# Attention with a gated mixer: the output projection of a head group moved into the next group, partial products added up in SBUF

## The chip, the core and the metric

One core of a Trainium2 chip. The metric is device time in microseconds (us); the kernel before takes 1070.64 us, the median of three runs (1069.9 to 1074.41). Engines: TensorE (PE in the profile, its weight loads PEld), VectorE (DVE), ScalarE (ACT), GpSimd (POOL), and SyncE (SP), which issues most DMAs.

## What is computed

The input x has 2048 tokens of 448 features. Two branches are mixed by a gate per token:

```python
g = sigmoid((x * gate_w).sum(-1))
q = (x @ wq) as 16 heads of 28;  k = x @ wk;  v = x @ wv      # one k and v for all heads
a = concat_heads(softmax(q k^T / sqrt(28)) v) @ wo
h = gelu(layernorm(x) @ w1), its four quarters shifted by +1, -1, +2, -2 tokens
x1 = x + h_shifted @ w2
b = x1 + gelu(layernorm(x1) @ w3) @ w4
out = g * a + (1 - g) * b
```

## The kernel before

All arithmetic is kept near fp32 by splitting operands into a high and a low part (names ending in h and l): a product then takes three matmuls, high x high, high x low and low x high.

The work comes in stages. First k, v, the first two q and the mixer (to line 391), then the MLP (lines 393 to 450), then attention (from line 454), where this change lies. At the start of that last stage `gg` holds the gate g, and `x1` is scaled in place to (1 - g) * b (line 596).

**Units.** Attention runs over 16 groups `u` (NU = NB * NG): 4 blocks `b` of 512 query tokens, and in each 4 groups `g` of 4 heads. A group takes 16 key tiles `kt` of 128 keys; `k = u * 16 + kt` counts all of them. For each k the loop at line 646 issues four score matmuls ("s", line 663), one per head, each followed by ScalarE's exponential into SBUF ("p", line 665). After each odd k two tiles' worth of p, from two and three steps earlier, go through the "pv" matmuls (line 625), four heads side by side in one PSUM bank. The softmax sums come out of the same matmuls, from a column of ones beside v. So the loop repeats in pairs of key tiles: eight s, then a block of eight pv (sixteen in the trace, which records each twice).

**The order on TensorE** is written out by hand (`manual_schedule` for PE, line 59); the other engines' order is left to the scheduler. Side work is put between the score matmuls as *jobs*: generators in a list, of which `pump()` (line 601) advances the current one by one step, mostly one matmul, after every second score matmul (four times a pair), or after every one in the last group.

- `q_job(u + 2)` (line 493): eleven matmuls for the queries two groups ahead, put at the head of the list at kt = 2 (kt = 7 in group 0).
- `max_part`, `max_end`, `max_rows` for group u + 1 (called directly at kt 6 to 11): "m", four small matmuls that estimate each row's maximum, reduced by the DVE (line 167), and the small "mt" (line 193).
- When a group's pv is done (at kt = 1 of the next), `recip_begin` copies it to SBUF (o), fetches its sums through a DMA (rt), takes the reciprocal on the DVE and sends it to `rb` by two DMAs. `norm_job` (line 541) is queued for k + 6, counted from the group's last kt: a matmul "rbc" (line 543) spreads the reciprocals over the partitions, the DVE multiplies (line 545), and POOL splits the result into onh and onl (lines 548 and 549; five buffers each, "onh" and "onl").
- After the last group of a block, four `wo_job`s (line 567), one for each 128 tokens, are queued for k + 8. Each adds up the block's output projection in **one PSUM tile** over all four groups, 4 x 3 matmuls ("wo", `wo_group`, lines 556, 558, 560); then `gate_out` (line 562) does out = psum * g + x1 on the DVE (line 564) and stores it.
- The last block is different. Its groups 0 and 1 are queued at the start of the last group (line 650) and its group 2 at its middle (line 632), into four PSUM tiles `wo_last` that stay open to the end; two of them take banks of the score tiles, so that in the last group `s_tile(n, True)` goes round three banks and not five (line 478). Its group 3 is done in the tail (`tail_c`, line 708).

**PSUM banks.** Eight: two "mm", two "s" and one "misc" hold score tiles; one "mx" holds pv; two "m" (`misc_tile` = `m_tile`, line 466) are shared by m, mt, q, rbc and wo. A tile waits until the reader of the bank's earlier tile is done.

The branch at line 734 recomputes everything if a softmax sum came out too large; it isn't entered here.

Of the kernel before, what the change touches and what calls it, by code (L numbers as in the profile page):

```python
# [8 lines left out]
F32 = mybir.dt.float32  # L9
F32R = mybir.dt.float32r  # L10
AF = mybir.ActivationFunctionType
ALU = mybir.AluOpType
# [3 lines left out]
P = 128  # L16
S = 2048
D = 448
# [4 lines left out]
NB = S // 512  # L23
NT = S // P
NF = F // P
NG = H // 4
# [9 lines left out]
def f32(ap):  # L36
    return ap.bitcast(F32)
# [3 lines left out]
def gated_mix_kernel(  # L41
# [13 lines left out]
    nc = tc.nc  # L55
# [11 lines left out]
    x1 = keep.tile([P, NT, D], F32, name="x1")  # L67
# [3 lines left out]
    gg = keep.tile([P, NT], F32, name="gg")  # L71
# [20 lines left out]
    def misc_tile(name):  # L92
        return psA.tile([P, 512], F32, tag="misc", bufs=1, name=name)
# [59 lines left out]
    NU = NB * NG  # L153
# [4 lines left out]
    def max_tile(name):  # L158
        return psA.tile([P, 512], F32, tag="mx", bufs=1, name=name)
# [294 lines left out]
    with tc.tile_pool(name="s3", bufs=1, reuse_waits="tile") as s3, \  # L454
# [8 lines left out]
        woh = s3.tile([P, 4, D], F32R, name="woh")  # L463
# [11 lines left out]
        def s_spare(name):  # L475
            return psA.tile([P, 512], F32, tag="misc", bufs=1, name=name)

        def s_tile(n, last=False):
            return (mm_tile, mm_tile, s_spare, s_more, s_more)[n % (3 if last else 5)](f"s_{n}")

        xact = {}

# [31 lines left out]
        on_of = {}  # L514
# [24 lines left out]
            return o, rb  # L539

        def norm_job(u, o, rb):
            ps = (mm_tile if u == NU - 2 else misc_tile)(f"rbc_{u}")
            nc.tensor.matmul(ps, sel8, rb, start=True, stop=True)
            on = s3.tile([P, 512], F32, tag="onf", bufs=2, name=f"on_{u}")
            nc.vector.tensor_mul(on, o, ps)  # L545
            onh = s3.tile([P, 512], F32R, tag="onh", bufs=5, name=f"onh_{u}")
            onl = s3.tile([P, 512], F32R, tag="onl", bufs=5, name=f"onl_{u}")
            nc.gpsimd.tensor_copy(onh, on)  # L548
            nc.gpsimd.tensor_tensor(onl, on, f32(onh), ALU.subtract)
            on_of[u] = (onh, onl)  # L550
            yield

        def wo_group(ps, b, t, g, first, last):
            tok = slice(t * P, (t + 1) * P)
            onh, onl = on_of[b * NG + g]
            nc.tensor.matmul(ps, onh[:, tok], woh[:, g, :], start=first, stop=False)  # L556
            yield
            nc.tensor.matmul(ps, onh[:, tok], wol[:, g, :], start=False, stop=False)  # L558
            yield
            nc.tensor.matmul(ps, onl[:, tok], woh[:, g, :], start=False, stop=last)  # L560

        def gate_out(n, ps):
            ot = s3.tile([P, D], F32, tag="ot", bufs=3, name=f"ot_{n}")
            nc.vector.scalar_tensor_tensor(ot, ps, gg[:, n:n + 1], x1[:, n, :], op0=ALU.mult, op1=ALU.add)  # L564
            nc.sync.dma_start(out[0, n * P:(n + 1) * P, :], ot)

        def wo_job(b, t):
            ps = misc_tile(f"wo_{b}_{t}")[:, 0:D]
            for g in range(NG):
                yield from wo_group(ps, b, t, g, g == 0, g == NG - 1)  # L570
                if g < NG - 1:
                    yield
            gate_out(4 * b + t, ps)
            yield

        wqraw = s3.tile([P, 4, 512], F32, tag="raw", bufs=2, name="wqraw")
        nc.sync.dma_start(wqraw, wq)
# [20 lines left out]
        jobs = []  # L598
# [13 lines left out]
        def drain():  # L612
            while current[0] is not None or jobs:
                pump()
# [3 lines left out]
        def pv_group(k):  # L618
            u, kt = divmod(k, NT)
            if kt == 0:  # L620
                pv_of[u] = max_tile(f"pv_{u}")
            pv = pv_of[u]
            ps = p_of.pop(k)
            for j in range(4):
                nc.tensor.matmul(pv[32 * j:32 * j + 32, :], vext[:, kt, :], ps[j],  # L625
                                 start=(kt == 0), stop=(kt == NT - 1), tile_position=(0, 32 * j))
            if kt == NT - 1 and u < NU - 1:
                o, rb = recip_begin(u, pv_of.pop(u))
                delayed.append((k + 6, lambda: norm_job(u, o, rb)))
                if u == NU - 2:  # L630
                    for t in range(4):
                        delayed.append((k + 10, lambda t=t: wo_last_job(t, NG - 2)))
                elif u % NG == NG - 1:
                    for t in range(4):
                        delayed.append((k + 8, lambda t=t: wo_job(u // NG, t)))

        wo_last = []

        def wo_last_job(t, g):
            if g == 0:  # L640
                wo_last.append((m_tile if t < 2 else s_more)(f"wo_{NB - 1}_{t}")[:, 0:D])
            yield from wo_group(wo_last[t], NB - 1, t, g, g == 0, False)
            yield

        delayed = []
        for k in range(NU * NT + LAG):
            u, kt = divmod(k, NT)
            while delayed and delayed[0][0] <= k:
                jobs.append(delayed.pop(0)[1])
            if k == (NU - 1) * NT:  # L650
                for g in range(NG - 2):
                    for t in range(4):
                        jobs.append(lambda t=t, g=g: wo_last_job(t, g))
            if k < NU * NT:
                if kt == (7 if u == 0 else 2) and u + 2 < NU:
                    jobs.insert(0, lambda u=u: q_job(u + 2))
                if kt == 8 and (u + 3) % NG == 0 and u + 3 < NU:
                    load_x((u + 3) // NG)
                p_of[k] = []
                for j in range(4):  # L660
                    n = 4 * k + j
                    ps = s_tile(n, u == NU - 1)
                    nc.tensor.matmul(ps, kS[0:98, kt * P:(kt + 1) * P], q_of[u][0:98, j, :], start=True, stop=True)  # L663
                    p = s3.tile([P, 512], F32, tag="p", bufs=4 * (LAG + PVB) + 2, name=f"p_{n}")
                    nc.scalar.activation(p, ps, AF.Exp, scale=SCALE)  # L665
                    p_of[k].append(p)
                    if j % 2 == 1 or u == NU - 1:
                        pump()
                if u + 1 < NU:
                    if 6 <= kt < 10:  # L670
                        max_part(u + 1, kt - 6, m_tile)
                    elif kt == 10:
                        max_end(u + 1)
                    elif kt == 11:
                        max_rows(u + 1, m_tile)
            if k >= LAG and k % PVB == PVB - 1:
                for kk in range(k - LAG - PVB + 1, k - LAG + 1):
                    if kk >= 0:
                        pv_group(kk)
        assert not delayed  # L680
        drain()

        u = NU - 1
        pv = pv_of.pop(u)
        o = s3.tile([P, 512], F32, tag="o", bufs=2, name=f"o_{u}")
        onh = s3.tile([P, 512], F32R, tag="onh", bufs=5, name=f"onh_{u}")
        onl = s3.tile([P, 512], F32R, tag="onl", bufs=5, name=f"onl_{u}")
        on_of[u] = (onh, onl)
        toks = [slice(t * P, (t + 1) * P) for t in range(4)]
        on4 = {}  # L690
# [15 lines left out]
            nc.vector.tensor_sub(onl[:, toks[t]], tq, f32(onh)[:, toks[t]])  # L706

        def tail_c(t):
            for _ in wo_group(wo_last[t], NB - 1, t, NG - 1, False, True):
                pass  # L710
            gate_out(4 * (NB - 1) + t, wo_last[t])

        for t in range(4):
            nc.scalar.copy(o[:, toks[t]], pv[:, toks[t]])
# [19 lines left out]
        with tc.If(again > 0):  # L734
            for b in range(NB):
                load_x(b)
                for g in range(NG):
                    u = b * NG + g
                    for _ in q_job(u):
                        pass  # L740
                    max_full(u, m_tile)
                    max_end(u)
                    max_rows(u, m_tile)
                    pv = max_tile(f"pv2_{u}")
                    for kt in range(NT):
                        for j in range(4):
                            ps = mm_tile(f"s2_{u}_{kt}_{j}")
                            nc.tensor.matmul(ps, kS[0:98, kt * P:(kt + 1) * P], q_of[u][0:98, j, :],
                                             start=True, stop=True)
                            p = s3.tile([P, 512], F32, tag="p", bufs=4 * (LAG + PVB) + 2, name=f"p2_{u}_{kt}_{j}")  # L750
                            nc.scalar.activation(p, ps, AF.Exp, scale=SCALE)
                            nc.tensor.matmul(pv[32 * j:32 * j + 32, :], vext[:, kt, :], p,
                                             start=(kt == 0), stop=(kt == NT - 1), tile_position=(0, 32 * j))
                    for _ in norm_job(u, *recip_begin(u, pv, False)):
                        pass
                for t in range(4):
                    for _ in wo_job(b, t):
                        pass


_OUTS = [((1, S, D), "float32")]
# [48 lines left out]
```

## Time and profile before

| | |
|---|---|
| median of 3 runs | 1070.64 us (1069.9 to 1074.41) |
| the profiled execution | 1070.98 us |
| its span in the profile | 1069.1 us |
| TensorE busy | 1039.7 us, 97% |
| ScalarE busy | 673.2 us, 63% |
| VectorE busy | 258.0 us, 24% |
| GpSimd busy | 159.8 us, 15% |
| TensorE's granted clock, mean | 0.987 |

A row of the profile gives the line in the kernel, the engine, the operation, what it writes and reads, the shapes, how often (x), the busy time and the mean in ns of one, and the idle time ahead of it with what ended it. The "chain of waits" is followed back from the last instruction: at each step to what released it. Its rows "in order of time" give start, duration and what, of stretches merged, of which a long window lists only the longest. A "timeline" lists instructions in order of time, alike ones merged. Matmuls overlap, and their ends are modelled: the spacing of two starts tells what one costs.

### The profile page before, as it was taken

What the parts mean: (1) busy time and instruction counts of PE and PEld (TensorE: products, weight loads), DVE (VectorE), ACT (ScalarE), POOL (GpSimd) and SP (SyncE); (2) the same over time, 40 slices, a digit from 0 to 9 for tenths busy, and PEclk for the clock granted to TensorE, in tenths of its full rate; (3) what the DMA queues carried; (4) which work ended last, traced back from release to release, by engine and by line L of the source; (5) the groups of instructions that cost most, each with busy time, mean ns of one, the idle gap of its engine ahead of it and who ended that gap; (6) DMA issues with size and microseconds to landing.
All of it is one profiled execution on the core that took longest, in us unless ns stands there. A gap on an engine that the chain in (4) does not pass through costs nothing.

```text
span 1069.1 us, 13948 instructions
## 1 busy us (share of the span) xinstructions
PE 1039.7 (97%) x5610; PEld 679.6 (64%) x5610; DVE 258.0 (24%) x521; ACT 673.2 (63%) x1318; POOL 159.8 (15%) x182
## 2 busy tenths in 40 slices
PE   6999889999999999999999999999999999999995
PEld 4787778888888888454554555554655555555542
DVE  6744952311411311401110110120110210111102
ACT  5444451222222223788888888889888889888873
POOL 5622430110200201603000002010002100000100
PEclk9999899999999999999999999999999999999998
DMA  9401330000000000423211202220202220211001
GB/s 312 131 1 37 111 111 1 1 1 1 1 1 1 1 1 29 164 32 70 33 17 16 31 20 40 39 31 3 39 10 41 39 31 2 40 24 26 10 2 38
DMA packets 30541, 41.15 MB, mean 38 GB/s; under 512 B 8004, under 2 KB 20100, under 8 KB 30340
## 3 DMA queue, kind: packets, MB, share of 16 engines
q1 hardware_dynamic: 30324, 40.04, 16.3%
q8 instruction: 46, 0.75, 0.3%
q14 instruction: 27, 0.22, 0.1%
q10 hardware_dynamic: 144, 0.13, 0.1%
HBM read 23.28 MB, written 3.67 MB: 25 GB/s over the span
## 4 chain that ended last, share of the span: by engine, by line
PE 91%; DVE 4%; DMA 1%; ACT 1%; POOL 1%; issue 1%; SPq 0%; POOLq 0%; ACTq 0%; DVEq 0%
PE s L663 27%; PE pv L625 22%; PE acc L420 4%; PE acc L419 4%; PE acc L421 4%; PE g L115 4%; PE g L116 4%; PE g L117 4%; PE q L503 3%; PE m L166 2%; PE wo L560 1%; PE wo L558 1%; PE wo L556 1%; PE g L119 1%; PE g L118 1%; PE h L116 1%
## 5 line engine op out<-in xcount | busy, mean ns | idle before, releaser
L665 ACT ACTIVATE p<-s 128x512 f32<-128x512 f32 x1024 | 517.6, 627 | 98.1 <-PE s L663 97.8
L663 PE MATMUL s<-qs,kS 98*128 98x512 f32 x1024 | 343.6, 420 | 1.4 <-ACT p L665 0.7
L663 PEld LDWEIGHTS s<-qs,kS 98*128 98x128 f32 x1024 | 181.6, 189 | 168.2 <-ACT p L665 127.1
L625 PE MATMUL pv<-p,vext 128*32 128x512 f32 x2048 | 247.6, 602 | 0.0
L409 ACT ACTIVATE gh<-g 128x512 fp32r<-128x512 f32 x56 | 33.6, 600 | 174.9 <-PE g L119 174.9
L625 PEld LDWEIGHTS pv<-p,vext 128*32 128x32 f32 x2048 | 53.7, 109 | 107.6 <-issue 100.3
L411 DVE TENSOR_TENSOR gl<-gf,gh 128x512 fp32r<-128x512 f32 x56 | 41.3, 738 | 192.1 <-ACT gf L410 192.0
L419 PE MATMUL acc<-w4h,gh 128*128 128x448 f32 x224 | 82.6, 369 | 0.0
L420 PE MATMUL acc<-w4l,gh 128*128 128x448 f32 x224 | 82.0, 366 | 0.0
L421 PE MATMUL acc<-w4h,gl 128*128 128x448 f32 x224 | 81.7, 365 | 0.0
L167 DVE TENSOR_REDUCE mr<-m 128x4 f32<-128x512 f32 x64 | 44.3, 692 | 146.0 <-PE m L166 145.3
L548 POOL CAST onh<-on 128x512 fp32r<-128x512 f32 x15 | 9.2, 614 | 414.8 <-DVE on L545 228.7
L115 PE MATMUL g<-ah,w3h 128*128 128x512 f32 x168 | 67.1, 399 | 3.1 <-ACT gf L410 2.8
L116 PE MATMUL g<-al,w3h 128*128 128x512 f32 x168 | 66.5, 396 | 0.1
L117 PE MATMUL g<-ah,w3l 128*128 128x512 f32 x168 | 66.3, 394 | 0.0
L521 DVE SCALAR_TENSOR_TENSOR good<-rt,good 128x16 f32<-128x16 f32 x15 | 2.6, 175 | 190.2 <-DMA rt<-o 190.2
L419 PEld LDWEIGHTS acc<-w4h,gh 128*128 128x128 f32 x224 | 42.0, 188 | 4.9
L420 PEld LDWEIGHTS acc<-w4l,gh 128*128 128x128 f32 x224 | 42.1, 188 | 4.8
L421 PEld LDWEIGHTS acc<-w4h,gl 128*128 128x128 f32 x224 | 42.0, 188 | 3.6
L166 PEld LDWEIGHTS m<-kS,qs 96*128 96x128 f32 x256 | 38.4, 191 | 6.3 <-DVE mr L167 1.2
L115 PEld LDWEIGHTS g<-ah,w3h 128*128 128x128 f32 x168 | 31.9, 190 | 9.7 <-ACT gf L410 3.3
L564 DVE SCALAR_TENSOR_TENSOR ot<-wo,gg,x 128x448 f32<-128x448 f32 x16 | 10.9, 682 | 108.0 <-PE wo L560 108.0
(204 smaller groups left out, 1144.4 us busy)
## 6 DMA issues: line engine op xcount, KB each, us to landing
qs<-qh SPq DMA_DIRECT2D x32, 256.0 KB
qs<-ql SPq DMA_DIRECT2D x16, 256.0 KB
xq<-in_xT_dram SPq DMA_DIRECT2D x4, 1024.0 KB
x<-in_x_dram SPq DMA_DIRECT2D x4, 896.0 KB
w3raw<-in_w_dram SPq DMA_DIRECT2D x7, 512.0 KB
out_dram<-ot SPq DMA_DIRECT2D x16, 224.0 KB
w4raw<-in_w_dram SPq DMA_DIRECT2D x7, 448.0 KB
xkv<-in_xT_dram SPq DMA_DIRECT2D x3, 1024.0 KB
```

Source lines behind the costliest of these rows:

```text
L115: nc.tensor.matmul(ps, wh[:, c, :], ah[:, c, :], start=(c == 0), stop=False)
L116: nc.tensor.matmul(ps, wh[:, c, :], al[:, c, :], start=False, stop=False)
L117: nc.tensor.matmul(ps, wl[:, c, :], ah[:, c, :], start=False, stop=False)
L166: nc.tensor.matmul(ps[:, j, :], q_of[u][0:96, j, t * P:(t + 1) * P], kS[0:96, 0:MK], start=True, stop=True)
L167: nc.vector.reduce_max(mx_of[u][:, :, t], ps, axis=AX.X)
L411: nc.vector.tensor_sub(gl, gf, f32(gh))
L419: nc.tensor.matmul(ps, gh[:, tok], w4h[i][:, k, :], start=(f == 0), stop=False)
L420: nc.tensor.matmul(ps, gh[:, tok], w4l[i][:, k, :], start=False, stop=False)
L421: nc.tensor.matmul(ps, gl[:, tok], w4h[i][:, k, :], start=False, stop=(f == NF - 1))
L625: nc.tensor.matmul(pv[32 * j:32 * j + 32, :], vext[:, kt, :], ps[j], start=(kt == 0), stop=(kt == NT - 1), tile_position=(0, 32 * j))
L663: nc.tensor.matmul(ps, kS[0:98, kt * P:(kt + 1) * P], q_of[u][0:98, j, :], start=True, stop=True)
L665: nc.scalar.activation(p, ps, AF.Exp, scale=SCALE)
```

## The change

Each group's output projection is done by itself, in the next group. `wo_job(u, t)` takes one group and 128 tokens: three matmuls into a PSUM tile of its own, then one DVE operation that multiplies by the gate and adds x1 (group 0 of a block) or the output tile so far (groups 1 to 3), in SBUF; after the fourth group the tile is stored. `norm_job` is no longer a job: its matmul is issued directly at kt = 6 of the next group, ahead of that step's scores, and four `wo_job`s are queued at kt = 8. The last block is treated like the others, so that the last group has five score banks and pumps after every second score matmul. The tail does only the last group's four jobs. There are five "ot" tiles, and two buffers each for onh and onl.

```diff
-        def s_tile(n, last=False):
-            return (mm_tile, mm_tile, s_spare, s_more, s_more)[n % (3 if last else 5)](f"s_{n}")
+        def s_tile(n):
+            return (mm_tile, mm_tile, s_spare, s_more, s_more)[n % 5](f"s_{n}")
...
         def norm_job(u, o, rb):
-            ps = (mm_tile if u == NU - 2 else misc_tile)(f"rbc_{u}")
+            ps = misc_tile(f"rbc_{u}")
...
-            onh = s3.tile([P, 512], F32R, tag="onh", bufs=5, name=f"onh_{u}")
-            onl = s3.tile([P, 512], F32R, tag="onl", bufs=5, name=f"onl_{u}")
+            onh = s3.tile([P, 512], F32R, tag="onh", bufs=2, name=f"onh_{u}")
+            onl = s3.tile([P, 512], F32R, tag="onl", bufs=2, name=f"onl_{u}")
...
-        def wo_group(ps, b, t, g, first, last):
+        ot_of = {}
+
+        def wo_job(u, t, tile_of=misc_tile):
+            b, g = divmod(u, NG)
+            n = 4 * b + t
             tok = slice(t * P, (t + 1) * P)
-            onh, onl = on_of[b * NG + g]
-            nc.tensor.matmul(ps, onh[:, tok], woh[:, g, :], start=first, stop=False)
+            onh, onl = on_of[u]
+            ps = tile_of(f"wo_{u}_{t}")[:, 0:D]
+            nc.tensor.matmul(ps, onh[:, tok], woh[:, g, :], start=True, stop=False)
             yield
             nc.tensor.matmul(ps, onh[:, tok], wol[:, g, :], start=False, stop=False)
             yield
-            nc.tensor.matmul(ps, onl[:, tok], woh[:, g, :], start=False, stop=last)
-
-        def gate_out(n, ps):
-            ot = s3.tile([P, D], F32, tag="ot", bufs=3, name=f"ot_{n}")
-            nc.vector.scalar_tensor_tensor(ot, ps, gg[:, n:n + 1], x1[:, n, :], op0=ALU.mult, op1=ALU.add)
-            nc.sync.dma_start(out[0, n * P:(n + 1) * P, :], ot)
-
-        def wo_job(b, t):
-            ps = misc_tile(f"wo_{b}_{t}")[:, 0:D]
-            for g in range(NG):
-                yield from wo_group(ps, b, t, g, g == 0, g == NG - 1)
-                if g < NG - 1:
-                    yield
-            gate_out(4 * b + t, ps)
-            yield
+            nc.tensor.matmul(ps, onl[:, tok], woh[:, g, :], start=False, stop=True)
+            before = x1[:, n, :] if g == 0 else ot_of[n]
+            if g == 0:
+                ot_of[n] = s3.tile([P, D], F32, tag="ot", bufs=5, name=f"ot_{n}")
+            nc.vector.scalar_tensor_tensor(ot_of[n], ps, gg[:, n:n + 1], before, op0=ALU.mult, op1=ALU.add)
+            if g == NG - 1:
+                nc.sync.dma_start(out[0, n * P:(n + 1) * P, :], ot_of[n])
...
                 o, rb = recip_begin(u, pv_of.pop(u))
-                delayed.append((k + 6, lambda: norm_job(u, o, rb)))
-                if u == NU - 2:
-                    for t in range(4):
-                        delayed.append((k + 10, lambda t=t: wo_last_job(t, NG - 2)))
-                elif u % NG == NG - 1:
-                    for t in range(4):
-                        delayed.append((k + 8, lambda t=t: wo_job(u // NG, t)))
...
+                norms.append((u, o, rb))
+
+        norms = []
         for k in range(NU * NT + LAG):
             u, kt = divmod(k, NT)
-            while delayed and delayed[0][0] <= k:
-                jobs.append(delayed.pop(0)[1])
-            if k == (NU - 1) * NT:
-                for g in range(NG - 2):
-                    for t in range(4):
-                        jobs.append(lambda t=t, g=g: wo_last_job(t, g))
+            if norms and kt == 6:
+                for _ in norm_job(*norms[0]):
+                    pass
+            if norms and kt == 8:
+                v = norms.pop()[0]
+                for t in range(4):
+                    jobs.append(lambda t=t, v=v: wo_job(v, t))
...
-                    ps = s_tile(n, u == NU - 1)
+                    ps = s_tile(n)
...
-                    if j % 2 == 1 or u == NU - 1:
+                    if j % 2 == 1:
                         pump()
...
         def tail_c(t):
-            for _ in wo_group(wo_last[t], NB - 1, t, NG - 1, False, True):
+            for _ in wo_job(u, t, m_tile if t < 2 else s_more):
                 pass
-            gate_out(4 * (NB - 1) + t, wo_last[t])
```

In the changed kernel the three output matmuls stand at lines 561, 563 and 565, the DVE's addition at 569, the store at 571, the pv matmuls at 622, the score matmuls at 647 and the exponentials at 649.

More of the change, by code (lines that the diff above doesn't have):

```diff
@@ L679, in gated_mix_kernel @@
                         pv_group(kk)
-        assert not delayed
+        assert not norms
         drain()
@@ L685, in gated_mix_kernel @@
         o = s3.tile([P, 512], F32, tag="o", bufs=2, name=f"o_{u}")
-        onh = s3.tile([P, 512], F32R, tag="onh", bufs=5, name=f"onh_{u}")
-        onl = s3.tile([P, 512], F32R, tag="onl", bufs=5, name=f"onl_{u}")
+        onh = s3.tile([P, 512], F32R, tag="onh", bufs=2, name=f"onh_{u}")
+        onl = s3.tile([P, 512], F32R, tag="onl", bufs=2, name=f"onl_{u}")
         on_of[u] = (onh, onl)
```

13 lines of the change are left out of this document (3 added, 10 removed).

## The prediction

> **What bounds the kernel now.** I read the page's chain first, then the chain in order of time over the attention loop (lines 646 to 679), where the change lies.
>
> ```profile
> PE 91%; DVE 4%; DMA 1%; ACT 1%; POOL 1%; issue 1%; SPq 0%; POOLq 0%; ACTq 0%; DVEq 0%
> ...
> L564 DVE SCALAR_TENSOR_TENSOR ot<-wo,gg,x 128x448 f32<-128x448 f32 x16 | 10.9, 682 | 108.0 <-PE wo L560 108.0
> ```
>
> The path is TensorE's; the DVE is on it for 4%, and the addition that the change multiplies costs it 682 ns apiece. So the count of additions matters little by itself. What matters is where TensorE's matmuls stand, and whether one of them waits for such an addition.
>
> The loop repeats in pairs of key tiles: eight score matmuls with jobs let in between, then one block of sixteen pv matmuls. In the chain in order of time (start, duration, what) the pv blocks are therefore a clock: from the start of one to the next is one pair. Two stretches in group 7 (a group is one `u`, eight pairs):
>
> ```profile
> 703.41 1.85 PE pv L625 x16
> 708.27 1.85 PE pv L625 x16
> 713.73 1.85 PE pv L625 x16
> 718.70 1.85 PE pv L625 x16
> ```
>
> ```profile
> 723.21 1.85 PE pv L625 x16
> 725.06 2.59 PE s L663 x8
> 727.65 1.85 PE pv L625 x16
> ```
>
> Read the differences. A pair with four q matmuls takes 4.86 us (703.41 to 708.27); with three q and two maximum parts of four small matmuls each ("m"), 5.46; with one rbc and the two m parts, 4.97; an empty pair 4.44 (723.21 to 727.65). The empty pair is shorter by only 0.42 for four matmuls less, though one costs 0.24 (below): there ScalarE's exponentials hold it, and the first jobs of a pair are partly free. That is what the change can win or lose: output matmuls put where room is.
>
> Pairs with output matmuls, from groups 8 and 14:
>
> ```profile
> 757.14 1.85 PE pv L625 x16
> 761.94 1.85 PE pv L625 x16
> 763.79 0.67 PE s L663 x2
> 766.69 1.85 PE pv L625 x16
> ```
>
> ```profile
> 981.55 1.85 PE pv L625 x16
> ...
> 987.14 1.85 PE pv L625 x16
> ```
>
> Four output matmuls and the small mt: 4.80. Four alone: 4.75. Four and two m parts: 5.59.
>
> The ends of the stretches that change, first the block ahead of group 1, then the last group:
>
> ```profile
> 461.78 1.85 PE pv L625 x16
> ```
>
> ```profile
> 1005.75 1.85 PE pv L625 x16
> ...
> 1044.56 1.85 PE pv L625 x16
> 1047.52 2.45 PE s L663 x5
> 1049.98 3.69 PE pv L625 x32
> ```
>
> Groups 1 to 14 take 1005.75 - 461.78 = 543.97. The last group's first seven pairs take 38.81, or 5.54 each: they carry 36 output matmuls and have only three score banks (`last=True`). Its last pair, without any job, takes 5.42 (1044.56 to 1049.98) for want of those banks.
>
> **The change part by part.** *Nothing leaves TensorE.* Both kernels issue 192 output matmuls, 15 rbc, the same q, m and mt. They move. Every group from 1 on now has this order: pair 1 empty, pairs 2 and 3 four q each, pair 4 rbc at its head with three q and two m, pair 5 four output and two m, pair 6 four output and mt, pair 7 four output, pair 8 empty. Each of four output jobs takes three pumps, so twelve fill pairs 5 to 7.
>
> Groups 1 to 13, each, without any wait: 4.44 + 4.86 + 4.86 + 5.70 + 5.59 + 4.80 + 4.75 + 4.44 = 39.44, where 5.70 is the 5.46 pair and one rbc more at 0.24 (the row of it is below). Thirteen make 512.72. Group 14 has no q: 3 x 4.44 + 4.97 + 5.59 + 4.80 + 4.75 + 4.44 = 37.87. Together 550.59 against 543.97: **+6.62**.
>
> Group 15 has neither q nor m and five score banks again: 3 x 4.44, one with rbc at its head 4.44 + 0.24 = 4.68 (at the head it delays the first score, so I take it in full; pumped it might be free), 3 x 4.75: 32.25 against 38.81, **-6.56**. Last pair 4.44 against 5.42: **-0.98**. The tail behind it has the same matmuls, additions and stores.
>
> So the rearranged matmuls alone give -0.92: what the last group sheds is paid again in the groups before it, since a pair filled with four costs the same wherever it is.
>
> *The new wait.* The output tiles take turns with m, rbc, q and mt in two PSUM banks ("m", bufs=2), and each is now read out by the DVE after three matmuls, not twelve. Following each tile to the instruction that frees its bank, one place is tight in groups 1 to 14: pair 5, where the fourth m part takes the bank of the first output tile. The nearest picture of that pair is TensorE's timeline in group 10 and the DVE's beside it (start, duration, engine, line, operation):
>
> ```profile
> 834.09 0.56 PE L166 MATMUL m<-kS,qs 96*128 96x128 f32 x4
> 834.49 0.68 PE L663 MATMUL s<-qs,kS 98*128 98x512 f32 x2
> 835.00 0.37 PE L558 MATMUL wo<-wol,onh 128*128 128x448 f32 x1
> 835.21 0.63 PE L663 MATMUL s<-qs,kS 98*128 98x512 f32 x2
> 835.68 0.37 PE L560 MATMUL wo<-woh,onl 128*128 128x448 f32 x1
> 835.88 0.56 PE L166 MATMUL m<-kS,qs 96*128 96x128 f32 x4
> ```
>
> ```profile
> 834.69 0.69 DVE L167 TENSOR_REDUCE mr<-m 128x4 f32<-128x512 f32 x1 [1.77 <-PE m L166]
> 836.48 0.69 DVE L167 TENSOR_REDUCE mr<-m 128x4 f32<-128x512 f32 x1 [1.10 <-PE m L166]
> 837.21 0.18 DVE L185 TENSOR_SCALAR mc<-mr 128x16 fp32r<-128x16 f32 x1
> ```
>
> Put T = 834.09, the third m part. In the changed order the output matmul at T + 0.91 is the first tile's last, the one at T + 1.59 opens the second tile, and the m part at T + 1.79 wants the first tile's bank. How soon the addition starts behind its last matmul, the tail shows:
>
> ```profile
> 1056.31 0.36 PE L560 MATMUL wo<-woh,onl 128*128 128x448 f32 x1
> ...
> 1056.71 0.68 DVE L564 SCALAR_TENSOR_TENSOR ot<-wo,gg,x 128x448 f32<-128x448 f32 x1
> ```
>
> 0.40 later. So it starts at T + 1.31; the DVE has just finished the reduction (834.69 + 0.69 is T + 1.29). It ends at T + 1.99. What such a wait looks like, and how soon TensorE goes on, one place of the last group shows:
>
> ```profile
> 1029.69 0.40 PE L543 MATMUL rbc<-rb,sel 128*128 128x512 f32 x1
> 1029.93 0.40 PE L663 MATMUL s<-qs,kS 98*128 98x512 f32 x1
> 1030.94 0.73 PE L663 MATMUL s<-qs,kS 98*128 98x512 f32 x2 [0.61 <-DVE on L545]
> ```
>
> (The spacing of the first two rows is the 0.24 of a matmul.) The m part is due at T + 1.79 and free to go no earlier than T + 1.99: 0.20 at the least. With its weights, due one matmul ahead and behind the same wait, it is up to 0.20 + 0.20 = 0.40 and a semaphore's way. I take **0.36**, near the upper end, because the row above shows a wait for a DVE result going into TensorE's time in full. Pair 5 has no room: it is the second fullest. Queued behind the waiting m part are the pv block and the next pair's scores, so ScalarE waits too. 14 x 0.36 = **+5.04** (ends: 0 if the DVE is quicker than the rows, 14 x 0.6 = 8.4 with the 0.61 of the row above).
>
> A sentence of the Trainium skill speaks here: Perfetto Trace Analysis, section Matmuls, says that independent matmul groups should rotate through PSUM banks so that reading one out overlaps the next group's matmuls. By it the wait would be nothing; the rows above agree for every hand-over but this one, where two banks serve two streams at once.
>
> *At nothing.* 48 more additions are 48 x 0.682 = 33 us of DVE, beside TensorE's work; without that cover each would cost its wait as above. The second tile's first matmul (due T + 1.59) wants the bank whose reduction ends at T + 1.29: margin 0.3, for its weights 0.1. mt wants the second tile's bank, six matmuls or 1.4 us behind that tile's last; the addition is done 0.40 + 0.68 = 1.08 behind: margin 0.3. The fourth tile wants mt's bank, copied during the pv block between. rbc now runs at the head of pair 4 instead of as a job behind q: its inputs are sent by SP in pair 1, two pairs of 4.86 earlier; m takes its bank seven matmuls later. On POOL, onh and onl now stand ahead of the load_x casts, which wait for the last q matmul anyway. SP's order keeps rt, rb, qs and mrow; the four stores of a block stand behind additions of pairs 5 to 7, before the next group's rt, and nothing behind them is due sooner. The fewer onh/onl buffers are released by matmuls two groups back.
>
> **Sum.** -0.92 + 5.04 = +4.1 on the profiled execution's 1070.98 (span 1069.1 and 1.9 around it): 1075.1. That execution lies 0.34 over the median 1070.64, so for a median: **1074.7**, +0.4%. A measurement of this kernel tells about 0.5% (5.3 us) from no change.
>
> **The rivals.**
>
> *The read-out is hidden* (the skill's rule, as a mechanism): the addition starts a little sooner, or pair 5's matmuls go slower than in group 10, and the bank is free when m comes. For it: the lack is only 0.2 to 0.4 us of a 5.59 pair. Against: the DVE is busy until T + 1.29 and the addition cannot start before its matmul has drained. Time 1070.64 - 0.92 = 1069.7.
>
> *The hand-over is longer than the rows say*, which ends slower: one mechanism, the DVE's queue in pairs 5 and 6. If reduction and addition behind each other cost 0.25 us more than I have put, the m part waits 0.61: 14 x 0.61 - 0.92 = +7.6, 1078.2; from there the margins of 0.3 at the second tile and at mt are used up too, and each further 0.1 costs three places, 14 x 0.3 = 4.2 us (1082 at 0.35). For it: the addition now reads and writes the same SBUF tile. Against: 837.21 follows 836.48 + 0.69 by 0.04, so the DVE starts one result behind another at once. The Trainium skill, VectorE: DVE Perf Modes, section The DRAIN you can't avoid, says that after an operation a drain of about its duration less 266 ns passes before the next; as an estimate 0.42 more for a 0.69 reduction, and this rival in full. The trace's 0.04 disagrees, and I go by it.
>
> *The filling is cheaper than its rows*: if the output matmuls of pairs 6 and 7 were free in 14 groups, each pair would return 0.31 to 0.36, about 9.4 us, and the time would be 1065.3. Against: 4.75 and 4.80 are measured for just these pairs.
>
> That the change doesn't do what it says can't be: the built order has four output jobs in each group from 1 on.
>
> **How the numbers follow.** Forecast (1072 to 1078) 0.65; hidden read-out 0.15; longer hand-over 0.13; cheaper filling 0.04; something unnamed 0.03. The range 1069.3 to 1079.0 takes the forecast with both ends of the wait, the hidden read-out, and the start of the longer hand-over. Faster by over 0.5% (below 1065.3) 0.04. Slower (above 1076.0): the longer hand-over and about a quarter of the forecast's own spread, 0.29. Within 0.5%: 0.67.
>
> **What would show it.** Right: pairs 5 of groups 1 to 14 at 5.9 to 6.0, with a TensorE wait at L166 on the DVE's line 569, about fourteen times 0.2 to 0.5; groups 1 to 13 at 39.8, against 543.97 / 14 = 38.9 on the mean before; group 15 at 32; the last pair at 4.4. Wrong: waits for line 569 at 561 or at mt (longer hand-over), pairs 6 and 7 at 4.4 (cheaper filling), no wait at L166 (hidden), or a wait at 543 for its small transfers, which I put at nothing.

## The result, and the profile after

The changed kernel takes 1076.65 us (median of 19 runs, 1072.97 to 1079.09) against 1072.33 (19 runs, 1069.0 to 1074.41) for the kernel before on the same chips: a ratio of 1.0048 with a 95% interval of 1.0038 to 1.0059. It is slower by about 5 us, and the forecast was +4.1. (With more runs the median of before has come out 1.7 us over the 1070.64 of the first three; that is why the forecast's 1074.7 lies 2 us under the time while its difference fits.) The profiled execution took 1078.19, with a span of 1076.3.

First the page of the changed kernel: the chain by engine, then the two groups of instructions that the forecast was about (line, engine, operation, tiles, count | busy us, mean ns | idle before and what ended it).

```profile
PE 89%; DVE 4%; DMA 3%; ACT 2%; POOL 1%; issue 1%; SPq 0%; POOLq 0%; ACTq 0%
...
L569 DVE SCALAR_TENSOR_TENSOR ot<-wo,gg,ot 128x448 f32<-128x448 f32 x48 | 32.8, 684 | 84.8 <-PE wo L565 84.5
...
L166 PEld LDWEIGHTS m<-kS,qs 96*128 96x128 f32 x256 | 37.4, 191 | 12.0 <-DVE ot L569 7.2
```

The DVE does 48 more additions for 33 us, and its share of the chain stays at 4%. But TensorE's weight load for a maximum's part (line 166) now waits for such an addition. TensorE's waits over groups 1 to 15 (who, for whom: us in total, times, the longest):

```profile
PEld m L166 <- DVE ot L569: 7.2, 14, 0.5
```

Fourteen times, once in each of groups 1 to 14, 0.5 us each. It is the only line of TensorE that waits for line 569 there. The rest of it is hidden, as the pv blocks show. Group 7 in the chain in order of time (start, duration, what), the same clock as in the prediction:

```profile
703.31 1.85 PE pv L622 x16
...
707.76 1.85 PE pv L622 x16
...
712.62 1.85 PE pv L622 x16
...
717.48 1.85 PE pv L622 x16
...
723.16 1.85 PE pv L622 x16
...
729.12 1.85 PE pv L622 x16
...
733.93 1.85 PE pv L622 x16
...
738.67 1.85 PE pv L622 x16
...
743.12 1.85 PE pv L622 x16
```

The differences are 4.45, 4.86, 4.86, 5.68, 5.96, 4.81, 4.74 and 4.45, in sum 39.81. The forecast was 4.44, 4.86, 4.86, 5.70, 5.95, 4.80, 4.75 and 4.44. Only the fifth is clearly longer than the pair of the same filling before (5.59). And the ends of the stretches, from the chain of the changed kernel:

```profile
464.52 1.85 PE pv L622 x16
...
1020.38 1.85 PE pv L622 x16
...
1052.72 1.85 PE pv L622 x16
...
1057.17 3.69 PE pv L622 x32
```

Groups 1 to 14 take 1020.38 - 464.52 = 555.86 (before 543.97, +11.89); the last group's first seven pairs 32.34 (before 38.81, -6.47); its last pair 4.45 (before 5.42, -0.97). The sum is +4.45 against a forecast of +4.1. The spans of the two profiled executions differ by 7.2; the other 2.74 lie ahead of 464.52 (461.78 before), where TensorE's order is the same in both kernels. The last section shows what that is.

### The profile page after: what moved, and what is told of

Its sections match the earlier page's. It is cut to its first block, busy times and chain, and to the rows that moved or that the text cites. A ratio compares the mean times of both kernels' runs of the same rounds, so it can differ in the third digit from the quotient of the medians.

```text
span 1076.3 us, 14021 instructions
## 1 busy us (share of the span) xinstructions
PE 1046.4 (97%) x5610; PEld 683.2 (63%) x5610; DVE 289.0 (27%) x569; ACT 673.0 (63%) x1318; POOL 160.4 (15%) x182
## 4 chain that ended last, share of the span: by engine, by line
PE 89%; DVE 4%; DMA 3%; ACT 2%; POOL 1%; issue 1%; SPq 0%; POOLq 0%; ACTq 0%
PE s L647 24%; PE pv L622 21%; PE acc L420 4%; PE acc L419 4%; PE acc L421 4%; PE g L115 4%; PE g L117 4%; PE g L116 4%; PE q L503 3%; PE m L166 2%; PE g L119 1%; PE g L118 1%; PE h L116 1%; PE wo L563 1%; PE wo L565 1%; PE h L117 1%
## 5 line engine op out<-in xcount | busy, mean ns | idle before, releaser
L647 PE MATMUL s<-qs,kS 98*128 98x512 f32 x1024 | 337.7, 418 | 0.5 <-ACT p L649 0.5
L569 DVE SCALAR_TENSOR_TENSOR ot<-wo,gg,ot 128x448 f32<-128x448 f32 x48 | 32.8, 684 | 84.8 <-PE wo L565 84.5
L166 PE MATMUL m<-kS,qs 96*128 96x128 f32 x256 | 37.6, 269 | 1.9 <-DVE mr L167 0.5
```

The costliest lines, as they stand in the source:

```text
L166: nc.tensor.matmul(ps[:, j, :], q_of[u][0:96, j, t * P:(t + 1) * P], kS[0:96, 0:MK], start=True, stop=True)
```

## The experiments

Nine kernels, each the changed kernel with the edit shown, and each timed beside the kernel before on the same chip. All the ratios below are to the kernel before; the changed kernel stands at 1.0048. Lengths of pairs are means over groups 1 to 13, taken in this section from the first score matmul of one pair to that of the next. By this clock rbc counts in pair 3, and the changed kernel's pairs 3 and 4 read 5.20 and 5.35; pair 5 is 5.95 by either. (Where the expectations speak of "eight transposes", they mean the eight small matmuls of two maximum parts.)

| run | median us (runs) | ratio to before, 95% | pairs 1 to 8 | a group |
|---|---|---|---|---|
| the change | 1076.65 (19) | 1.0048 [1.0038, 1.0059] | 4.45 4.85 5.20 5.35 **5.95** 4.80 4.74 4.45 | 39.80 |
| half an addition | 1074.27 (12) | 1.0021 [1.0005, 1.0037] | pair 5: **5.72** | 39.57 |
| two additions | 1085.88 (6) | 1.0132 [1.0111, 1.0153] | pair 5: **6.63** | 40.47 |
| no addition | 1072.76 (12) | 0.9991 [0.9976, 1.0006] | pair 5: **5.59** | 39.43 |
| jobs 1 tile later | 1065.02 (9) | 0.9946 [0.9928, 0.9964] | 4.45 4.85 5.20 5.35 5.16 4.81 4.75 4.45 | 39.02 |
| jobs 2 later | 1070.27 (12) | 0.9982 [0.9971, 0.9994] | 4.45 4.84 5.20 5.35 4.85 5.18 4.75 4.74 | 39.36 |
| jobs 2 later, q earlier | 1063.16 (6) | 0.9923 [0.9904, 0.9942] | 4.84 4.87 4.97 4.74 4.85 5.17 4.74 4.74 | 38.92 |
| jobs 1 later, q earlier | 1059.84 (4) | 0.9882 [0.9863, 0.9901] | 4.85 4.86 4.97 4.74 5.18 4.80 4.75 4.45 | 38.60 |
| three score banks | 1086.48 (5) | 1.0140 [1.0118, 1.0162] | as the change | 39.79 |
| jobs of 12 and 13 late | 1075.23 (12) | 1.0027 [1.0016, 1.0038] | as the change to group 12 | |

### Is it the wait? Three lengths of one addition

My theory (A) was the wait; its rival (B) that the new packing of pair 5 is that long of itself. The runs change how long the first output tile's bank is held, and leave TensorE's order alone.

```diff
-            nc.vector.scalar_tensor_tensor(ot_of[n], ps, gg[:, n:n + 1], before, op0=ALU.mult, op1=ALU.add)
+                if t == 0:
+                    nc.gpsimd.memset(ot_of[n][:, 224:D], 0.0)
+            w = 224 if t == 0 else D
+            nc.vector.scalar_tensor_tensor(ot_of[n][:, 0:w], ps[:, 0:w], gg[:, n:n + 1], before[:, 0:w],
+                                           op0=ALU.mult, op1=ALU.add)
```

> This kernel adds only 224 of the 448 columns of the first of a block's four output tiles (the other half of that tile stays zero, a part of the output that is left out); TensorE's work and its order are those of the changed kernel. Theory A, the wait: pair 5 of groups 1 to 14 lasts 5.95 us because the fourth part of the maximum waits for that addition; the addition then takes about 0.36 us in place of 0.68, the bank comes free some 0.3 us earlier, the waits at L166 on the addition go to 0.1 us or less each, pair 5 goes to 5.60 to 5.70, and the time falls by 14 x 0.3 = 4 us to about 1072.5, the time of before. Theory B, the packing: pair 5 is long because a pair with four output matmuls and eight transposes is that long in this order, and the wait only stands beside it: pair 5 stays at 5.9 or more and the time at 1076.5.

Measured: pair 5 5.72, ratio 1.0021, 2.9 us less than the change. The sign is A's, the size smaller than expected. Why, the timelines tell. Group 7 of the changed kernel, TensorE and then the DVE (start, duration, engine, line, operation, count; in brackets the idle time before):

```profile
726.39 0.56 PE L166 MATMUL m<-kS,qs 96*128 96x128 f32 x4
...
727.30 0.38 PE L565 MATMUL wo<-woh,onl 128*128 128x448 f32 x1
...
727.99 0.37 PE L561 MATMUL wo<-woh,onh 128*128 128x448 f32 x1
728.45 0.66 PE L166 MATMUL m<-kS,qs 96*128 96x128 f32 x4
729.05 1.92 PE L622 MATMUL pv<-p,vext 128*32 128x512 f32 x16
```

```profile
726.98 0.69 DVE L167 TENSOR_REDUCE mr<-m 128x4 f32<-128x512 f32 x1 [2.11 <-PE m L166]
727.71 0.69 DVE L569 SCALAR_TENSOR_TENSOR ot<-wo,gg,ot 128x448 f32<-128x448 f32 x1
```

With T = 726.39 the last matmul of the first tile is at T + 0.91, the addition starts at T + 1.32 and ends at T + 2.01, the fourth part goes at T + 2.06, the pv block at T + 2.66. The same place with half an addition:

```profile
726.03 0.56 PE L166 MATMUL m<-kS,qs 96*128 96x128 f32 x4
...
727.86 0.66 PE L166 MATMUL m<-kS,qs 96*128 96x128 f32 x4
728.45 1.93 PE L626 MATMUL pv<-p,vext 128*32 128x512 f32 x16
```

```profile
727.36 0.45 DVE L572 SCALAR_TENSOR_TENSOR ot<-wo,gg,ot 128x224 f32<-128x224 f32 x1
```

Half the columns take 0.45 us and not 0.36, so the bank is free some 0.24 sooner. The part goes at T + 1.83 (0.23 sooner), the pv block at T + 2.42 (0.24): the pair gives back all that the addition does. A wait of the weight load is left: 0.3 us, fourteen times, where at most 0.1 was expected.

Two additions:

```diff
+            if t == 0:
+                twice = s3.tile([P, D], F32, tag="twice", bufs=1, name=f"twice_{u}")
+                nc.vector.scalar_tensor_tensor(twice, ps, gg[:, n:n + 1], before, op0=ALU.mult, op1=ALU.add)
             nc.vector.scalar_tensor_tensor(ot_of[n], ps, gg[:, n:n + 1], before, op0=ALU.mult, op1=ALU.add)
```

> The addition of the first output tile of each block is preceded by an equal one into a tile that nobody reads, so that its bank is held by 0.68 us more; TensorE's work and its order are those of the changed kernel. Theory A, the wait: the bank is due before it is free, so every bit of the hold is added in full: pair 5 of groups 1 to 14 goes from 5.95 to about 6.6 us, the waits at L166 on the addition grow by 0.6 to 0.7 each, and the time by 14 x 0.65 = 9 us to about 1086. Theory B, the packing, or a wait with slack behind it (a pair that is also held by ScalarE's exponentials): pair 5 grows by less than 0.2 and the time by less than 3 us.

The weight load's wait for it in that kernel (there line 572):

```profile
PEld m L166 <- DVE ot L572: 16.7, 14, 1.2
```

It grew from 0.5 to 1.2 us, pair 5 from 5.95 to 6.63 (most groups 6.67): 0.68 for an addition of 0.69. The ratio rose by 0.0084, 9.0 us. B's "under 3 us" is out.

And none, which also isolates the step of the prediction that the rearranged matmuls alone give -0.92 us:

```diff
+            if t == 0 and u < NU - 1:
+                if g == 0:
+                    nc.gpsimd.memset(ot_of[n], 0.0)
+            else:
+                nc.vector.scalar_tensor_tensor(ot_of[n], ps, gg[:, n:n + 1], before, op0=ALU.mult, op1=ALU.add)
-            nc.vector.scalar_tensor_tensor(ot_of[n], ps, gg[:, n:n + 1], before, op0=ALU.mult, op1=ALU.add)
```

> The additions of the first output tile of each block are left out for all groups but the last (its output is then only the last group's product; this part of the output is left out); TensorE's work and order are those of the changed kernel, and nothing reads the bank that the fourth part of the maximum takes over. It tests the step that without the wait the new order costs what the pairs of the before profile say, 0.92 us less than before. If so: no wait at L166 on the addition, pair 5 at 5.59 us, 14 x 0.36 = 5.0 us less than the changed kernel, about 1071.6, within 0.3% of before. If the new order itself is dearer: pair 5 stays at 5.7 or more, as with half an addition (5.72), and the time at 1074 or more, 0.3% over before.

Group 7 of this kernel, TensorE's timeline:

```profile
727.06 0.56 PE L166 MATMUL m<-kS,qs 96*128 96x128 f32 x4
...
728.87 0.56 PE L166 MATMUL m<-kS,qs 96*128 96x128 f32 x4
729.36 1.92 PE L626 MATMUL pv<-p,vext 128*32 128x512 f32 x16
```

No wait: the part goes at T + 1.81 and the pv block at T + 2.30. Pair 5 is 5.59, the length of the like pair before. So the hand-over costs 2.66 - 2.30 = 0.36, in two pieces: 0.25 until the fourth part starts (T + 2.06 for T + 1.81), and 0.11 behind it, since its four small matmuls then need 0.60 until pv in place of 0.49. The first piece is the wait for the bank. The second is the part's first weight load, here in TensorE's timeline of the changed kernel:

```profile
728.45 0.52 PEld L166 LDWEIGHTS m<-kS,qs 96*128 96x128 f32 x4 [0.51 <-DVE ot L569]
```

and in that of the kernel without the addition:

```profile
728.66 0.62 PEld L166 LDWEIGHTS m<-kS,qs 96*128 96x128 f32 x4
```

Without the wait this load starts 0.21 ahead of its matmul (728.66 and 728.87), beside the matmul before it; with the wait both start at 728.45, and the load is no longer covered. With half an addition the first piece is nearly gone (T + 1.83) and the second stays, which is why that run did not reach 5.6. The ends of the stretches in the chain of the kernel without the addition:

```profile
467.46 1.85 PE pv L626 x16
...
1018.06 1.85 PE pv L626 x16
...
1050.41 1.85 PE pv L626 x16
1054.85 3.69 PE pv L626 x32
```

550.60 for groups 1 to 14 (forecast without the wait: 550.59), 32.35 and 4.44. Against before that is 6.63 - 6.46 - 0.98 = -0.81, and the ratio 0.9991 is 1.0 us under before by its middle, with an interval from -2.6 to +0.6.

### Is it the place? Two ways to move the jobs

The wait hangs on which tile is the next in that bank, so moving the output jobs by one key tile should remove it, at no cost in work.

```diff
-            if norms and kt == 8:
+            if norms and kt == 9:
```

> The output jobs enter the queue one key tile later (at the tenth instead of the ninth), so that pair 5 carries two output matmuls in place of four and none of its maximum's parts takes the bank of a tile just finished; the work is the same. Theory A with the lengths of the before profile: pair 5 (two output matmuls and eight transposes) about 5.2 us in place of 5.95, pair 6 4.80, pair 7 4.75, pair 8 (two output matmuls in a pair that ScalarE's exponentials hold at 4.44) 4.45 to 4.60; per group 0.65 to 0.75 less, 9 to 10 us in all, about 1067, under the time of before. Theory B, that the output matmuls cost what they cost wherever they stand: what pair 5 loses pair 8 gains, 4.44 to 5.0, and the time stays within 3 us of 1076.5.

It came out as the pairs said, with a little more gain than expected: pair 5 with two output matmuls 5.16, pair 8 with two 4.45, a group 39.02, 14 x 0.78 = 10.9 us less than the change; the ratio fell by 0.0102, 10.9 us. No line of TensorE waits for the addition. Of the 0.78, 0.37 is the wait (39.80 against 39.43 without the addition); the other 0.41 comes from two output matmuls that went from a pair that counts them (5.59 without wait) to one that the exponentials hold at 4.44 to 4.45, where they cost nothing. This version is faster than before.

Two key tiles later, and the query jobs earlier (the expectations below call this the spread kernel):

```diff
-            if norms and kt == 8:
+            if norms and kt == 10:
...
-                if kt == (7 if u == 0 else 2) and u + 2 < NU:
+                if kt == (7 if u == 0 else 0) and u + 2 < NU:
```

> The output jobs enter the queue two key tiles later (at the eleventh), and the query job of each group but the first two key tiles earlier (at the first), so that the query matmuls lie in pairs 1 to 3, the maximum's parts alone in pairs 4 and 5, and the output matmuls in pairs 6 to 8; the work is the same. If ScalarE's exponentials hold a pair at 4.44 and only what exceeds it counts: pairs 1 to 3 about 4.85, 4.85, 5.2 with the broadcast of the reciprocals behind them, pairs 4 and 5 about 4.75, pair 6 4.80 or with a new wait of the maximum's last tile up to 5.15, pairs 7 and 8 4.75 each: 38.5 a group in place of 39.8, 14 to 18 us less than the changed kernel, about 1060. If the filling of TensorE alone counts (theory B), the sum of matmuls is the same and the time stays within 3 us of 1076.5.

1063.16: of the two branches for pair 6 the dearer held, 5.17. TensorE's waits in groups 1 to 15 of this kernel have one row for line 569:

```profile
PEld mt L193 <- DVE ot L569: 7.2, 14, 0.5
```

It is the same hand-over at another tile: mt is due a little too early for the first output tile's bank, and pays 0.5 us of wait and 0.36 of pair (5.17 for 4.81), as m did. The group is 38.92 and not 38.5 for this and for a slip of mine: the pairs listed there add to 38.7 without a wait, 39.05 with it. To separate the two edits, the first alone (`kt == 10`, queries where the change has them):

> Only the later half of the edit of the spread kernel: the output jobs enter the queue two key tiles later, the query jobs stay where they are. If the hand-over of a bank costs what it costs wherever the next tile is due: the wait moves to the last tile of the maximum (L193), which is due behind the second output tile's first matmul; pair 5 (eight transposes alone) about 4.85, pair 6 5.17 with that wait, pairs 7 and 8 4.75 each: 39.36 a group against 39.81 in the changed kernel and 39.02 with one key tile; 6 us less than the changed kernel, about 1070.5. If the exponentials cover that wait because this pair stands near their 4.44: pair 6 4.80, 39.0 a group, about 1065.

39.36 a group, as written there, and ratio 0.9982. And the cheaper of each:

```diff
-            if norms and kt == 8:
+            if norms and kt == 9:
...
-                if kt == (7 if u == 0 else 2) and u + 2 < NU:
+                if kt == (7 if u == 0 else 0) and u + 2 < NU:
```

> The two cheaper halves together: the output jobs one key tile later and the query jobs two key tiles earlier. If each pair costs by what lies in it (4.44 where the exponentials hold it): 4.84, 4.87, 4.97, 4.74, 5.16, 4.81, 4.75, 4.45, 38.6 a group against 38.92 in the spread kernel, 14 x 0.33 = 4.6 us less than that, about 1058.5, 1.2% under before. If the gains don't add up, because the spread kernel's wait at the last tile of the maximum was covered by the exponentials: 1063.

38.60 a group, 1059.84, ratio 0.9882. The four combinations add up: the queries earlier are worth 0.44 a group with the jobs at 10 (39.36 to 38.92) and 0.42 with the jobs at 9 (39.02 to 38.60). The group that begins behind 693.97, in the chain in order of time:

```profile
693.97 1.85 PE pv L622 x16
...
698.81 1.85 PE pv L622 x16
...
728.10 1.85 PE pv L622 x16
...
732.55 1.85 PE pv L622 x16
```

Its first pair now has four q (4.84) and its last two output matmuls (4.45): no pair is empty, and it takes 38.58 where the changed kernel's group 7 takes 39.81. It is the fastest kernel of this study, 1.2% under before.

### What did the last group gain from?

The prediction took 6.56 us for the last group and 0.98 for its last pair, and set the first against the 24 output matmuls that it sheds. But the change gives it two score banks back as well. Matmuls (M) or banks (S)?

```diff
-        def s_tile(n):
-            return (mm_tile, mm_tile, s_spare, s_more, s_more)[n % 5](f"s_{n}")
+        def s_tile(n, last=False):
+            return (mm_tile, mm_tile, s_spare, s_more, s_more)[n % (3 if last else 5)](f"s_{n}")
...
-                    ps = s_tile(n)
+                    ps = s_tile(n, u == NU - 1)
```

> The changed kernel with the three score banks of before in the last group; its output matmuls stay where the change put them (twelve in that group). It asks what the change's gain in the last group comes from. Theory M, the matmuls moved out of it (the step that put 36 output matmuls at 38.81 us and 12 at 32.25): the pairs of the last group stay at 4.45 to 4.78, only the last pair takes 1 us more, and the time is about 1077.5. Theory S, the score banks given back: with three banks a pair lasts 5.4 us whatever lies in it (before, the last pair with no job took 5.42 and pairs with six output matmuls 5.43), so the last group's first seven pairs take 38 to 39 us in place of 32.36, its last pair with the tail 13.3 in place of 12.4, and the time rises by 6.5 to 7.5 us to about 1083.5.

The last group of this kernel in its chain:

```profile
1021.20 1.85 PE pv L622 x16
...
1026.62 1.90 PE pv L622 x16
...
1060.11 1.85 PE pv L622 x16
```

A pair with no job at all takes 5.42, and the seven pairs 38.91, with 12 output matmuls; before, they took 38.81, with 36. So the gain came from the banks, and the matmuls had been free where they stood: before, a pair with six took 5.43. They aren't free in every order: in this kernel a pair with four, let in after every second score and not after every one, takes 5.63. The ratio puts this kernel 9.9 us over the change, where 6.5 to 7.5 were expected; its profiled execution was 7.8 over, 7.0 of it from the last group on, and what the runs have beyond that stays open. What three banks do, ScalarE's and TensorE's timelines of the third pair show:

```profile
1034.47 4.03 ACT L649 ACTIVATE p<-s 128x512 f32<-128x512 f32 x8 [1.41 <-PE s L647]
```

```profile
1032.07 1.92 PE L622 MATMUL pv<-p,vext 128*32 128x512 f32 x16
1033.93 0.98 PE L647 MATMUL s<-qs,kS 98*128 98x512 f32 x3
1035.12 2.45 PE L647 MATMUL s<-qs,kS 98*128 98x512 f32 x5 [0.21 <-ACT p L649]
```

While TensorE does a pv block (1.92) ScalarE runs out of the scores laid up for it and stands still for 1.41, until the next score; TensorE fills its three banks and then waits for ScalarE to release one. With five banks ScalarE has scores for longer. The changed kernel, second and third pair:

```profile
1026.75 0.59 ACT L525 COPY o<-pv 128x512 f32<-128x512 f32 x1
...
1031.68 4.03 ACT L649 ACTIVATE p<-s 128x512 f32<-128x512 f32 x8 [0.42 <-PE s L647]
```

ScalarE's stand is 0.42, and the 0.99 between the two is what a pair gains (5.43 to 4.44).

The reverse test puts the matmuls back and leaves the banks:

```diff
+        late = []
...
+            if k == (NU - 1) * NT:
+                for v in late:
+                    for t in range(4):
+                        jobs.append(lambda t=t, v=v: wo_job(v, t))
+                late.clear()
...
             if norms and kt == 8:
-                v = norms.pop()[0]
-                for t in range(4):
-                    jobs.append(lambda t=t, v=v: wo_job(v, t))
+                late.append(norms.pop()[0])
+                if u < NU - 3 or u == NU - 1:
+                    for v in late:
+                        for t in range(4):
+                            jobs.append(lambda t=t, v=v: wo_job(v, t))
+                    late.clear()
```

> The changed kernel with the output jobs of heads' groups 12 and 13 held back to the start of the last group, so that it carries 36 output matmuls as before, but with five score banks. Groups 13 and 14 lose their twelve each: 38.05 in place of 39.81 and 36.7 in place of 38.44, 3.5 us less together. Theory S, the score banks: a pair with four output matmuls takes 4.75 here as elsewhere, the last group's first seven pairs about 33.7 in place of 32.36, its last pair 0.3 more, and four matmuls that find no pair 0.9 behind it: 1 us less than the changed kernel, about 1075.5. Theory M: 36 output matmuls make the last group 38.8 again, 3 us more than the changed kernel, about 1079.7.

(onh and onl have four buffers each here.) The last group in its chain:

```profile
1015.46 1.85 PE pv L622 x16
...
1020.22 1.85 PE pv L622 x16
...
1048.98 1.85 PE pv L622 x16
```

Pairs with four output matmuls take 4.76, the first seven 33.52 with 28 of the 36; four more lie in the last pair (4.76 too) and four behind it. The ratio is 1.0027, less than the change's by 0.0021 with intervals that touch. S again: nothing of M's 38.8.

## Why the prediction was right, and where not

**The new wait** (0.36 in pair 5, 14 times, +5.04). Right in place, count and size: 14 waits at line 166, 555.86 against 550.60 without the addition, 5.26 or 0.376 each. Its parts: T + 1.31 to T + 1.99 was forecast for the addition, T + 1.32 to T + 2.01 measured. Of "0.20 at the least, up to 0.40 with its weights" the bank took 0.25 and the weights 0.11. That the 0.36 chosen between those bounds came within 0.02 is partly luck, since the choice rested on one row of another wait.

**Only this hand-over is tight.** Right: no wait at 561, mt or 543. It is near the edge all the same, as the two runs show that moved the jobs by two tiles and met the wait at mt.

**The rearranged matmuls alone** (-0.92). The sum was right (-0.81 by pairs, ratio 0.9991). Groups 1 to 14 came out to the hundredth (+6.62 forecast, +6.63) because small errors cancel: without the addition groups 1 to 13 take 39.43 each for 39.44, group 14 takes 38.08 for 37.87. Of these terms the last group's has the largest miss, -6.46 for -6.56, and it lies in the second pair: 4.54, where an empty pair's 4.44 was put and ScalarE also copies pv (0.59, the row above).

**The step that failed** in the reasoning is the sentence under that sum, "what the last group sheds is paid again in the groups before it, since a pair filled with four costs the same wherever it is". What the last group lost was not paid for by its matmuls: with three score banks its pairs took 5.4 us with six output matmuls or with none, so shedding them was worth nothing by itself, and getting the two banks back 38.91 - 32.34 = 6.57, with about 1 us more at the last pair. That the number held in spite of it is luck: the profile before has one row, 38.81, for both causes. By the sentence one would have expected the moved matmuls to be neutral; in truth 24 of them had been free where they stood, groups 1 to 14 take 6.6 us more in an order that has those 24 as well, and the banks paid for it.

**What the prediction didn't weigh**: that two output matmuls in an otherwise empty pair are free and four are not. It priced a pair with none (4.44) and with four (4.75); the same rows, asked where there is room, would have pointed to the two better orders.

**The rivals.** The hidden read-out (1069.7) is refuted by the waits and by the three lengths of the addition; the ratio without the addition, 0.9991, is where that rival would have lain. The cheaper filling (1065.3) is refuted by pairs 6 and 7 at 4.80 and 4.74. The longer hand-over (1078.2 or more) is refuted by the DVE's rows: the addition starts 0.04 behind the end of the reduction (726.98 + 0.69 to 727.71). The Trainium skill, VectorE: DVE Perf Modes, section The DRAIN you can't avoid, would have some 0.4 us of drain there, by the estimate in the prediction, but excepts a next operation that is not held; the trace of the changed kernel shows no such drain, as that of before did not.

**The size on the clock.** +4.45 by pairs, +5.1 by the ratio (its interval, 4.1 to 6.3, has the pairs in it and the forecast at its lower end). The ratio's middle stands at the 0.5% that I called no change: slower beyond doubt here, and of the size that one profile can't show by its span alone.

## What to carry to other kernels

When an accumulation in PSUM is replaced by additions elsewhere, the additions' total hardly counts (33 us of DVE here, hidden but for the hand-over); the time from a tile's last matmul to its bank's release does (here 0.41 to the start of the addition and 0.69 for it), at each place where the next tile in that bank is due sooner, and moving the jobs by one step can be worth more than the change. Fill the pairs that another engine holds first: here two output matmuls put into an empty pair were free (4.45), four were not (4.74). Before a gain is put down to work that moved away, look at which buffers moved with it: a stage starved of banks hides its other work, and undoing the banks alone tells the two apart in one run.

## What the runs showed of the hardware that I had not expected

Group 0 has the same order on TensorE in all these kernels, yet from its first score to group 1 it took between 39.6 and 43.1 us in the eleven profiles. Within it a stretch at a lower granted clock (0.73 to 0.84) comes at one of two places: in five profiles within the first two pairs, in six in the fourth, counted from the first score. Two stretches of the kernel before, then of the changed kernel (window, length, busy us and count of the engines, then PEclk, the granted clock):

```profile
423.94:433.79 9.85, 9.85 (x33) 3.40 (x31) 5.44 (x8) 7.95 (x16) 9.07 (x11) 0.84 0.60 213
...
438.31:443.58 5.27, 5.27 (x38) 3.19 (x34) 1.39 (x2) 4.14 (x9) 5.12 (x3) 1.00 0.39 149
```

```profile
425.08:433.35 8.27, 8.27 (x33) 3.22 (x32) 3.94 (x5) 7.84 (x16) 8.12 (x10) 1.00 0.70 254
...
437.80:446.30 8.50, 7.10 (x38) 3.48 (x34) 1.85 (x3) 4.14 (x9) 7.58 (x4) 0.80 0.53 163
```

In the kernel before the first stretch ran at 0.84 and took 9.85; in the changed one it ran in full (8.27), and the other, at 0.80, took 8.50 in place of 5.27. In 1.4 us of it (8.50 long, 7.10 busy) TensorE stood: a q matmul waited for POOL's split of the input (line 489). The net is 1.6 us of the 2.74 between the two profiles ahead of group 1; the other 1.1 is the attention's start, 425.08 against 423.94, behind work that is the same as well. Neither seems to have to do with the change, since four of the kernels made from the changed one have the low clock where the kernel before has it; both are of the size of the 5 to 6 us between the runs of one kernel, though only one execution of each was profiled. What sets the clock's place I have not tried.

A half addition (224 columns) took 0.45 us and a whole one (448) 0.69. If the time is a fixed part and one that goes with the columns, these two rows put the fixed part at 0.21, an estimate.
